# Output through VectorE transposes of 32x32 squares, in place of TensorE transposes; softmax weights normalised ahead of their split

## The chip, the cores and the metric

The kernel runs on one core of a Trainium2 chip. The metric is the device time of one execution in microseconds (us). The kernel before takes 1753.84 us, the median of 3 runs (1751.6 to 1754.51).

## The reference

Two stages run one after the other, in float32. The first is an induced attention in two steps, for 4 batches of 12480 tokens with 128 channels and 32 inducing rows. The second is a feed-forward layer with a squared ReLU, 128 to 2048 to 128.

```python
def mab(q, kv):
    s = scale * (q @ kv.transpose(0, 2, 1))
    s = s - s.max(-1, keepdims=True)
    a = np.exp(s)
    a /= a.sum(-1, keepdims=True) + 1e-09
    return a @ kv
h = mab(I, x)            # (4, 32, 128): the inducing rows attend to all tokens
y = mab(x, h)            # (4, 12480, 128): each token attends to the 32 rows of h
f = np.maximum(y @ w_in, 0.0)
out = (f * f) @ w_out    # 49920 tokens, 128 channels
```

## The kernel before, in words

**Units and blocks.** Each batch is cut into 13 units of 960 tokens, 52 units in all. A unit is two blocks (k = 0, 1) of 480 tokens, so the whole run has 104 blocks. Tokens lie along the free dimension in the feed-forward part, and channels lie on the 128 partitions.

**First.** For each unit, x is loaded to `xn` (120 partitions, 8 groups of 128 channels; line 383), turned to `xt` (128 channels x 960 tokens) by TensorE transposes (line 402), and evicted by ACT or DVE (`copy`, line 238). The scores of the 32 inducing rows, their running maximum and sum, and the running mix follow. When all units of a batch are done, `first_end` forms h and folds it into the first weight: `hw` = h times w_in, held as a high and a low part, so that the second attention and the first feed-forward matmul become one product.

**Second.** For each unit the 32 scores per token are formed (line 613), evicted (`ss`), turned (`s2t`, line 630), and then go through maximum, difference `d` and exponential (lines 637 to 644). The exponentials, not yet divided by their sum, are split into a high and a low part `sk` (lines 664 and 668), turned back (`ap`, line 675), evicted to `sw` (line 238, on ACT or DVE) and spread over 128 partitions by four transfers of the SP queue into `st` (line 690). The sum `z` goes another way: DVE sums it (line 648), POOL adds 1e-9 and squares it (lines 651 and 655), DVE inverts it (`zz`, line 659).

**The feed-forward block (`ffn_block`).** A block has four quads. A quad is four matmuls `h` from `st` (line 770), two ReLUs on ACT (`g`, line 778), one square on ACT (line 789), a high part `hi` and a low part `lo` on DVE (lines 793 and 797), and twelve matmuls into `op` (line 810): hi x wo_hi, hi x wo_lo, lo x wo_hi. One block therefore has 64 matmuls of 128x128 by 480. Since ReLU and square are homogeneous, the undivided weights make the result too large by z squared, which the end of the block takes out.

**The end of a block.** `op` (128 channels x 480 tokens, PSUM) is copied to `ot` by ACT or DVE (line 238), turned by four TensorE transposes to `otp` (line 830), multiplied by `zz` per token on DVE into `osb` (line 838), and once per unit stored by one transfer of 120 rows of 4096 bytes (line 845).

**What sets the order.** The whole program is written as tasks with an engine (or a choice `ACT|DVE`), an assumed duration, a due time, needs and buffers. `Plan.run` places them one after the other by these numbers, picks the engine where there is a choice, and the instructions are then issued in that order. Each engine executes its own queue in order. A changed task therefore moves others, and changes which engine the copies of line 238 go to. Two PSUM banks of kind `m` are shared by all narrow steps, and `ot`, `osb`, `st` and `sw` have two buffers each.

Of the kernel before, what the change touches and what calls it, by code (L numbers as in the profile page):

```python
# [154 lines left out]
def induced_attention_then_squared_relu_ffn(  # L155
# [448 lines left out]
    class Second:  # L604
# [6 lines left out]
        def score(self, where):  # L611
            for q in range(Q):
                nc.tensor.matmul(  # L613
                    where[q * M:(q + 1) * M, :], self.s["hT"][:, :M],
                    self.s["xt"][self.u][:, q * 2 * TS:(q + 1) * 2 * TS], start=True, stop=True,
                )

        def weigh(self, scored, where, bank_, due, step):
# [31 lines left out]
            def norm1():  # L650
                nc.gpsimd.tensor_scalar(v["z"], v["z"], 1e-9, 0.0, ALU.add, ALU.add)  # L651

            def norm2():
                v["zz"] = tiny.tile([TS, G, 1], F32, tag="z3", name=f"z3_{n}")
                nc.gpsimd.tensor_mul(v["zz"], v["z"], v["z"])  # L655

            def norm3():
# [1 line left out]
                nc.vector.reciprocal(s["zz", u], v["zz"])

# [43 lines left out]
            th = add("DVE", 210, high, d + 3 * step, [tp], port=True)  # L704
            tl = add("DVE", 335, low, d + 3 * step, [th], port=True)
            t = add("DVE", 330, total, d + 4 * step, [tp])
            t = add("POOL", 150, norm1, d + 5 * step, [t])
            t = add("POOL", 150, norm2, d + 5 * step, [t])
            self.zz = add("DVE", 120, norm3, d + 6 * step, [t])
            t = add("PE", 460, back, d + 4 * step, [tl], takes=[ba])  # L710
# [216 lines left out]
```

## Time and profile before

| | before |
|---|---|
| median of 3 runs | 1753.84 us (1751.6 to 1754.51) |
| profiled execution, first to last instruction | 1752.5 us |
| TensorE matmuls (PE) busy | 1724.4 us, 98% |
| VectorE (DVE) busy | 1666.2 us, 95% |
| ScalarE (ACT) busy | 1635.2 us, 93% |
| GpSimd (POOL) busy | 148.5 us, 8% |
| DMA, mean share of 16 engines (main queue) | 18.6%, 33416 packets |
| mean granted TensorE clock | 0.991 |

The profile gives one execution's span, and no separate time for that execution; the span lies 1.3 us under the median of the runs. Busy time of an engine is the time in which at least one of its instructions runs. Consecutive instructions on DVE overlap by some hundredths of a microsecond, so the means of the single instructions add up to more than the busy time. PE's matmul ends are modelled.

### The profile page before, as it was taken

What the parts mean: (1) busy time and instruction counts of PE and PEld (TensorE: products, weight loads), DVE (VectorE), ACT (ScalarE), POOL (GpSimd) and SP (SyncE); (2) the same over time, 40 slices, a digit from 0 to 9 for tenths busy, and PEclk for the clock granted to TensorE, in tenths of its full rate; (3) what the DMA queues carried; (4) which work ended last, traced back from release to release, by engine and by line L of the source; (5) the groups of instructions that cost most, each with busy time, mean ns of one, the idle gap of its engine ahead of it and who ended that gap; (6) DMA issues with size and microseconds to landing.
All of it is one profiled execution on the core that took longest, in us unless ns stands there. A gap on an engine that the chain in (4) does not pass through costs nothing.

```text
span 1752.5 us, 24391 instructions
## 1 busy us (share of the span) xinstructions
PE 1724.4 (98%) x9625; PEld 1418.5 (81%) x9625; DVE 1666.2 (95%) x1720; ACT 1635.2 (93%) x1677; POOL 148.5 (8%) x126
## 2 busy tenths in 40 slices
PE   7799999999999999999999999999999999999998
PEld 4488888888888888888888888888887888888886
DVE  6699999999999999999999999999999999999997
ACT  6599999999999999999999999999999999999997
POOL 1210010100100100100100100100110101010110
PEclk9699999999999999999999999999999999999999
DMA  9211211211121211211201211212101101010110
GB/s 236 64 46 34 57 46 34 57 46 37 44 57 35 57 45 39 63 36 46 68 23 46 53 38 46 57 34 50 42 24 34 35 23 46 24 45 24 35 35 23
DMA packets 33530, 82.46 MB, mean 47 GB/s; under 512 B 5032, under 2 KB 20424, under 8 KB 33416
## 3 DMA queue, kind: packets, MB, share of 16 engines
q1 hardware_dynamic: 33416, 80.91, 18.6%
q8 instruction: 76, 1.25, 0.3%
q14 instruction: 38, 0.31, 0.1%
HBM read 29.77 MB, written 25.56 MB: 32 GB/s over the span
## 4 chain that ended last, share of the span: by engine, by line
PE 95%; DMA 2%; DVE 1%; ACT 1%; issue 0%; SPq 0%; ACTq 0%; DVEq 0%
PE op L810 63%; PE h L770 21%; PE otp L830 3%; PE xtp L402 2%; PE na L613 2%; DMA words_i<-in_moe_w_in_dram 1%; PE ap L675 1%; PE nb L471 1%; PE wp L573 1%; PE na L417 1%; PE s2t L630 1%; PE ep L451 1%; DMA words_o<-in_moe_w_out_dram 0%; ACT g L778 0%; PE hp L471 0%
## 5 line engine op out<-in xcount | busy, mean ns | idle before, releaser
L797 DVE TENSOR_TENSOR lo<-g,hi 128x1920 fp32r<-128x1920 f32 x416 | 895.5, 2153 | 19.1 <-PE op L810 0.5
L778 ACT ACTIVATE g<-h 128x960 f32<-128x960 f32 x832 | 788.0, 970 | 53.1 <-PE h L770 44.4
L789 ACT ACTIVATE g<-g 128x1920 f32<-128x1920 f32 x416 | 755.6, 1816 | 9.7
L770 PE MATMUL h<-st,hw 128*128 128x480 f32 x1664 | 520.5, 386 | 2.5 <-DMA st<-sw 1.7
L793 DVE CAST hi<-g 128x1920 fp32r<-128x1920 f32 x416 | 479.4, 1152 | 23.8 <-ACT g L789 22.3
L810 PE MATMUL op<-hi,wo_hi 128*128 128x480 f32 x1664 | 477.8, 384 | 0.9 <-DVE hi L793 0.9
L810 PE MATMUL op<-lo,wo_hi 128*128 128x480 f32 x1664 | 471.1, 394 | 0.5 <-DVE lo L797 0.5
L810 PE MATMUL op<-hi,wo_lo 128*128 128x480 f32 x1664 | 431.7, 380 | 0.0
L770 PEld LDWEIGHTS h<-st,hw 128*128 128x128 f32 x1664 | 306.9, 188 | 65.8 <-ACT g L778 17.4
L810 PEld LDWEIGHTS op<-hi,wo_lo 128*128 128x128 f32 x1664 | 311.8, 188 | 50.9
L810 PEld LDWEIGHTS op<-hi,wo_hi 128*128 128x128 f32 x1664 | 305.2, 188 | 51.0 <-issue 1.8
L810 PEld LDWEIGHTS op<-lo,wo_hi 128*128 128x128 f32 x1664 | 292.9, 188 | 53.4 <-issue 11.8
L651 POOL TENSOR_SCALAR z<-z 120x8 f32<-120x8 f32 x52 | 89.6, 1723 | 1478.1 <-DVE z L648 1478.1
L838 DVE TENSOR_TENSOR osb<-otp,zz 120x512 f32<-120x512 f32 x104 | 71.3, 686 | 9.0 <-PE otp L830 8.8
L402 PE MATMUL xtp<-ident,xn 120*128 120x120 f32 x416 | 61.9, 273 | 5.8 <-DMA xn<-in_x_dram 4.8
L402 PEld LDWEIGHTS xtp<-ident,xn 120*128 120x128 f32 x416 | 49.8, 143 | 19.5 <-issue 5.8
L830 PE MATMUL otp<-ident,ot 128*120 128x128 f32 x416 | 62.4, 272 | 0.6 <-ACT ot L238 0.6
L830 PEld LDWEIGHTS otp<-ident,ot 128*120 128x120 f32 x416 | 50.9, 137 | 14.1 <-issue 1.4
L238 ACT COPY xt<-xtp 128x480 f32<-128x480 f32 x52 | 28.8, 559 | 14.3 <-PE xtp L402 13.6
L655 POOL TENSOR_TENSOR z<-z 120x8 f32<-120x8 f32 x52 | 37.7, 724 | 4.3
L675 PEld LDWEIGHTS ap<-identr,sk 120*128 120x128 f32 x208 | 31.3, 191 | 4.2 <-DVE hw L582 1.3
L238 DVE COPY ot<-op 128x480 f32<-128x480 f32 x53 | 34.5, 651 | 0.0
(94 smaller groups left out, 752.0 us busy)
## 6 DMA issues: line engine op xcount, KB each, us to landing
xn<-in_x_dram SPq DMA_DIRECT2D x52, 480.0 KB, 4.3
st<-sw SPq DMA_DIRECT2D x208, 120.0 KB, 2.3
out_dram<-osb SPq DMA_DIRECT2D x52, 480.0 KB, 3.3
words_i<-in_moe_w_in_dram SPq DMA_DIRECT2D x4, 512.0 KB, 10.2
words_o<-in_moe_w_out_dram SPq DMA_DIRECT2D x4, 512.0 KB, 7.6
ind_sb<-in_inducing_dram SPq DMA_DIRECT2D x1, 16.0 KB, 1.6
```

What stands on the lines that cost most here:

```text
L238: ENG[task.by](dst, src)
L402: nc.tensor.transpose(v["tp"][:, t * TS:(t + 1) * TS], self.xn[:, 4 * k + t, :], ident[:TS, :TS])
L651: nc.gpsimd.tensor_scalar(v["z"], v["z"], 1e-9, 0.0, ALU.add, ALU.add)
L675: nc.tensor.matmul(ap[:, q * TS:(q + 1) * TS], v["sk"][:, q].rearrange("t k a m -> t (k a m)"), identr[:TS, :TS], start=(q == 0), stop=(q ...
L770: nc.tensor.matmul(c["hp"][:, l, :BLK], s["hw"][:, f * P:(f + 1) * P], s["st", u][:, k, :], start=True, stop=True,)
L778: nc.scalar.activation(v["g"][:, 2 * i:2 * i + 2, :], c["hp"][:, :, :BLK], AF.Relu)
L789: nc.scalar.activation(v["g"], v["g"], AF.Square)
L793: nc.vector.tensor_copy(v["hi"], v["g"])
L797: nc.vector.tensor_sub(v["lo"], v["g"], v["hi"])
L810: nc.tensor.matmul(w["op"][:, :BLK], wo[:, 4 * j + l, :], v[name][:, l, :], start=(j == m == l == 0), stop=(j == NQ - 1 and m == 2 and l = ...
L830: nc.tensor.transpose(tp[:TS, q * P:(q + 1) * P], w["ot"][:, q * TS:(q + 1) * TS], ident)
L838: nc.vector.tensor_mul(s["osb", u].rearrange("t (q k) c -> t k q c", k=2)[:, k], w["tp"][:TS, :].rearrange("t (q c) -> t q c", q=Q), s["zz ...
```

## The change

It has four parts.

1. The x tokens are dealt to the partitions in another way. Before, partition p of a unit held 8 consecutive tokens, one piece of 4096 bytes. Now group j holds 120 consecutive tokens, so one load reads 8 pieces of 512 bytes per partition, and a block of 480 columns of `xt` is 480 consecutive tokens. The scores of the second attention read `xt` in two stretches of 120 columns for each matmul.
2. The softmax weights are divided by their sum ahead of their split: DVE adds 1e-9 to `z` (`safe`), inverts it (`invert`) and multiplies `d` by it (`share`, 120x256). The two POOL steps go, and one DVE reciprocal takes the place of another. The split, `ap`, `sw` and `st` now come behind these steps.
3. The end of a block is one DVE instruction: it transposes the 32x32 squares of `op` from PSUM into `rows` (128x480). The copy to `ot`, the four TensorE transposes and the multiplication by `zz` go.
4. The store of a block is four transfers, one for each group of 32 partitions. Each writes 480 pieces of 128 bytes: a quarter of the 512 bytes of each of 480 tokens. Before there was one transfer per unit.

```diff
-    XT, OT, ST = ("ACT|DVE", "ACT|DVE"), ("ACT|DVE", "ACT|DVE"), "ACT|DVE"
+    XT, ST = ("ACT|DVE", "ACT|DVE"), "ACT|DVE"
...
-    x_v = x.rearrange("b (p j) c -> b p j c", p=TS)
-    out_v = out.rearrange("(b p j) c -> b p j c", b=B, p=TS)
+    x_v = x.rearrange("b (u j p) c -> b u p j c", j=NT, p=TS)
+    out_v = out.rearrange("(b u k g r) (q c) -> b u k q r g c", b=B, u=NU, k=2, r=M, c=M)
...
-                nc.sync.dma_start(self.xn, x_v[b, :, u * NT:(u + 1) * NT, :])
+                nc.sync.dma_start(self.xn, x_v[b, u])
...
-                    where[q * M:(q + 1) * M, :], self.s["hT"][:, :M],
-                    self.s["xt"][self.u][:, q * 2 * TS:(q + 1) * 2 * TS], start=True, stop=True,
+                    where[q * M:(q + 1) * M, :].rearrange("m (k t) -> m k t", k=2), self.s["hT"][:, :M],
+                    self.s["xt"][self.u].rearrange("c (k q t) -> c q k t", k=2, q=Q)[:, q],
...
-            def norm1():
-                nc.gpsimd.tensor_scalar(v["z"], v["z"], 1e-9, 0.0, ALU.add, ALU.add)
-
-            def norm2():
-                v["zz"] = tiny.tile([TS, G, 1], F32, tag="z3", name=f"z3_{n}")
-                nc.gpsimd.tensor_mul(v["zz"], v["z"], v["z"])
-
-            def norm3():
-                s["zz", u] = tiny.tile([TS, G, 1], F32, tag="zz", name=f"zz_{n}")
-                nc.vector.reciprocal(s["zz", u], v["zz"])
+            def safe():
+                nc.vector.tensor_scalar_add(v["z"], v["z"], 1e-9)
+
+            def invert():
+                v["rz"] = tiny.tile([TS, G, 1], F32, tag="rz2", name=f"rz2_{n}")
+                nc.vector.reciprocal(v["rz"], v["z"])
+
+            def share():
+                nc.vector.tensor_mul(v["d"], v["d"], v["rz"].broadcast_to([TS, G, M]))
...
-        def done():
-            w["ot"] = att.tile([P, BLK], F32, tag="ot", name=f"ot_{n}")
-            copy(td, w["ot"], w["op"][:, :BLK])
-
-        def turn():
-            w["tp"] = tp = bank(f"otp_{n}")
+        def rows():
+            w["rows"] = att.tile([P, BLK // M, M], F32, tag="rows", name=f"rows_{n}")
+            nc.vector.transpose(w["rows"].rearrange("p g c -> p (g c)"), w["op"][:, :BLK])
+
+        def store():
             for q in range(Q):
-                nc.tensor.transpose(
-                    tp[:TS, q * P:(q + 1) * P], w["ot"][:, q * TS:(q + 1) * TS], ident
-                )
-
-        def turned():
...
-            nc.vector.tensor_mul(
-                s["osb", u].rearrange("t (q k) c -> t k q c", k=2)[:, k],
-                w["tp"][:TS, :].rearrange("t (q c) -> t q c", q=Q),
-                s["zz", u][:, k * Q:(k + 1) * Q].broadcast_to([TS, Q, C]),
-            )
-
-        def store():
-            nc.sync.dma_start(out_v[b, :, u * NT:(u + 1) * NT, :], s["osb", u])
...
+                nc.sync.dma_start(out_v[b, u, k, q], w["rows"][q * M:(q + 1) * M])
```

The plan moves other work with it. In the names below the first numbers are the unit and the block (and the quad), and the last number only counts tiles. Over the whole run, 14 of the copies to `xt` and 12 of the casts to `sw` go from DVE to ACT: DVE had 52 and 15 of them and has 38 and 3; ACT had 52 and 37 and has 66 and 49.

The first place is DVE while block 0 of unit 7 runs, where the softmax of unit 8 is finished (`d`, `z`, `zz` or `rz`, `sk`). Before:

```order
L664 CAST sk_8_3270<-d_8_3251 120x8x32
L838 TENSOR_TENSOR osb_6_3085<-otp_6_1_3261,zz_6_2711 120x4x128
L668 TENSOR_TENSOR sk_8_3270<-d_8_3251,sk_8_3270 120x8x32
L648 TENSOR_REDUCE z_0_8_3283<-d_8_3251 120x8
L797 TENSOR_TENSOR lo_7_0_2_3286<-g_7_0_2_3202,hi_7_0_2_3259 128x1920
L793 CAST hi_7_0_3_3312<-g_7_0_3_3255 128x1920
L238 COPY xt_9_3314<-xtp_9_0_3315 128x480
L659 RECIPROCAL zz_8_3333<-z_0_8_3325 120x8
L797 TENSOR_TENSOR lo_7_0_3_3335<-g_7_0_3_3255,hi_7_0_3_3312 128x1920
L793 CAST hi_7_1_0_3349<-g_7_1_0_3301 128x1920
```

Now:

```order
L644 TENSOR_REDUCE z_0_8_3225<-d_8_3212 120x8
L791 TENSOR_TENSOR lo_7_0_2_3230<-g_7_0_2_3153,hi_7_0_2_3216 128x1920
L647 TENSOR_SCALAR z_0_8_3225<-z_0_8_3225 120x8
L787 CAST hi_7_0_3_3247<-g_7_0_3_3210 128x1920
L651 RECIPROCAL rz_0_8_3260<-z_0_8_3225 120x8
L233 COPY xt_9_3249<-xtp_9_0_3250 128x480
L654 TENSOR_TENSOR d_8_3212<-d_8_3212,rz_0_8_3260 120x256
L791 TENSOR_TENSOR lo_7_0_3_3270<-g_7_0_3_3210,hi_7_0_3_3247 128x1920
L658 CAST sk_8_3288<-d_8_3212 120x8x32
L787 CAST hi_7_1_0_3290<-g_7_1_0_3243 128x1920
L662 TENSOR_TENSOR sk_8_3288<-d_8_3212,sk_8_3288 120x8x32
```

Before, the split `sk` followed the exponential at once, and the sum came behind it. Now the sum, `safe`, `invert` and `share` come first, with a `lo`, a `hi` and another `lo` between them, and the two steps of the split `sk` stand around the first `hi` of block 1.

The second place is PE from `ap` of unit 8 on, which opens the way of that unit's weights through `sw` and `st` to its first `h`. Before (the first `h_8` stands 14 rows behind the last row shown, 60 matmuls of 480 columns and three groups of transposes after `ap_8`):

```order
L675 MATMUL ap_8_3288<-identr,sk_8_3270 128x120 x4
L810 MATMUL op_7_0_3188<-hi_7_0_2_3259,wo_hi 128x480 x2
L810 MATMUL op_7_0_3188<-hi_7_0_2_3259,wo_lo 128x480 x4
L770 MATMUL h_7_1_1_3303<-st_7_2994,hw_881 128x480 x2
L402 MATMUL xtp_9_0_3315<-ident,xn_9_2847 128x120 x4
L810 MATMUL op_7_0_3188<-lo_7_0_2_3286,wo_hi 128x480 x4
L770 MATMUL h_7_1_2_3328<-st_7_2994,hw_881 128x480
L810 MATMUL op_7_0_3188<-hi_7_0_3_3312,wo_hi 128x480 x2
L770 MATMUL h_7_1_2_3328<-st_7_2994,hw_881 128x480
L810 MATMUL op_7_0_3188<-hi_7_0_3_3312,wo_hi 128x480 x2
L810 MATMUL op_7_0_3188<-hi_7_0_3_3312,wo_lo 128x480 x4
L770 MATMUL h_7_1_3_3346<-st_7_2994,hw_881 128x480 x2
```

Now:

```order
L669 MATMUL ap_8_3308<-identr,sk_8_3288 128x120 x4
L804 MATMUL op_7_1_3305<-hi_7_1_0_3290,wo_hi 128x480 x2
L804 MATMUL op_7_1_3305<-hi_7_1_0_3290,wo_lo 128x480 x4
L764 MATMUL h_7_1_5_3325<-st_7_3000,hw_881 128x480 x2
L804 MATMUL op_7_1_3305<-lo_7_1_0_3303,wo_hi 128x480 x4
L764 MATMUL h_7_1_6_3344<-st_7_3000,hw_881 128x480 x2
L804 MATMUL op_7_1_3305<-hi_7_1_1_3333,wo_hi 128x480 x4
L804 MATMUL op_7_1_3305<-hi_7_1_1_3333,wo_lo 128x480 x4
L764 MATMUL h_7_1_7_3360<-st_7_3000,hw_881 128x480 x2
L804 MATMUL op_7_1_3305<-lo_7_1_1_3347,wo_hi 128x480 x4
L764 MATMUL h_8_0_0_3370<-st_8_3327,hw_881 128x480 x2
```

`ap` has moved later by half a block: 28 matmuls of 480 columns stand between it and the first `h_8`. Over the 52 units this number is 27 to 45 in the first three batches (60 to 62 before), 24 or 32 in the last (64 to 66 before), and 20, 20 and 16 at the first units of the later batches (42, 38 and 41 before).

The third place is the queue of SP, which issues all transfers. Before:

```order
L690 DMA st_6_2683<-sw_6_2675 64x480 x4
L383 DMA xn_9_2847<-in_x_dram 120x1024
L845 DMA out_dram<-osb_5_2792 120x1024
L690 DMA st_7_2994<-sw_7_2983 64x480 x4
L383 DMA xn_10_3184<-in_x_dram 120x1024
L845 DMA out_dram<-osb_6_3085 120x1024
L690 DMA st_8_3305<-sw_8_3297 64x480 x4
```

Now:

```order
L684 DMA st_6_2692<-sw_6_2682 64x480 x4
L823 DMA out_dram<-rows_5_0_2718 32x15x32 x4
L378 DMA xn_9_2788<-in_x_dram 120x8x128
L823 DMA out_dram<-rows_5_1_2874 32x15x32 x4
L684 DMA st_7_3000<-sw_7_2991 64x480 x4
L823 DMA out_dram<-rows_6_0_3026 32x15x32 x4
L378 DMA xn_10_3137<-in_x_dram 120x8x128
L823 DMA out_dram<-rows_6_1_3161 32x15x32 x4
L684 DMA st_8_3327<-sw_8_3317 64x480 x4
```

Each block's store stands in the queue as four transfers. The store of block 1 stands ahead of the four `st` of the unit after the next, and the store of block 0 right behind them; a load of x stands between the two stores.

More of the change, by code (lines that the diff above doesn't have):

```diff
@@ L613, in score @@
                 nc.tensor.matmul(
-                    where[q * M:(q + 1) * M, :], self.s["hT"][:, :M],
-                    self.s["xt"][self.u][:, q * 2 * TS:(q + 1) * 2 * TS], start=True, stop=True,
+                    where[q * M:(q + 1) * M, :].rearrange("m (k t) -> m k t", k=2), self.s["hT"][:, :M],
+                    self.s["xt"][self.u].rearrange("c (k q t) -> c q k t", k=2, q=Q)[:, q],
+                    start=True, stop=True,
                 )
@@ L703, in weigh @@
             tp = add("ACT", 307, power, d + 2 * step, [td])
[L704 to L710, printed above, removed]
-            ts = add(ST, (455, 565), stacked, d + 5 * step, [t], takes=[bw], reads=[ba])
-            self.ready = add("SP", 1000, spread, d + 6 * step, [ts], takes=[self.bst], reads=[bw])
+            t = add("DVE", 330, total, d + 3 * step, [tp])
+            t = add("DVE", 70, safe, d + 3 * step, [t])
+            t = add("DVE", 115, invert, d + 3 * step, [t])
+            t = add("DVE", 340, share, d + 4 * step, [t], port=True)
+            th = add("DVE", 210, high, d + 4 * step, [t], port=True)
+            tl = add("DVE", 335, low, d + 5 * step, [th], port=True)
+            t = add("PE", 460, back, d + 5 * step, [tl], takes=[ba])
+            ts = add(ST, (455, 565), stacked, d + 6 * step, [t], takes=[bw], reads=[ba])
+            self.ready = add("SP", 1000, spread, d + 7 * step, [ts], takes=[self.bst], reads=[bw])
     def narrow(second, f, g, due, step, begun=None):
@@ L821, in ffn_block @@
             last = quad(j, last)
-        def done():
-            w["ot"] = att.tile([P, BLK], F32, tag="ot", name=f"ot_{n}")
-            copy(td, w["ot"], w["op"][:, :BLK])
-        def turn():
-            w["tp"] = tp = bank(f"otp_{n}")
-            for q in range(Q):
-                nc.tensor.transpose(
-                    tp[:TS, q * P:(q + 1) * P], w["ot"][:, q * TS:(q + 1) * TS], ident
-                )
-        def turned():
-            if k == 0:
-                s["osb", u] = att.tile([TS, NT, C], F32, tag="osb", name=f"osb_{b}_{u}")
-            nc.vector.tensor_mul(
-                s["osb", u].rearrange("t (q k) c -> t k q c", k=2)[:, k],
-                w["tp"][:TS, :].rearrange("t (q c) -> t q c", q=Q),
-                s["zz", u][:, k * Q:(k + 1) * Q].broadcast_to([TS, Q, C]),
-            )
-        def store():
-            nc.sync.dma_start(out_v[b, :, u * NT:(u + 1) * NT, :], s["osb", u])
-        bt = Buffer("m")
-        end = t0 + PERIOD / 2 + 8000
-        td = add(OT[k], (455, 570), done, end + 1500, [last], reads=[bo], late=LATE_OT)
-        t = add("PE", 420, turn, end + 3000, [td], takes=[bt])
-        t = s["out", u, k] = add("DVE", 600, turned, end + 4000, [t, second.zz], reads=[bt])
-        if k == 1:
-            add("SP", 2000, store, end + 6000, [t, s["out", u, 0]])
+        def rows():
+            w["rows"] = att.tile([P, BLK // M, M], F32, tag="rows", name=f"rows_{n}")
+            nc.vector.transpose(w["rows"].rearrange("p g c -> p (g c)"), w["op"][:, :BLK])
+        def store():
+            for q in range(Q):
+                nc.sync.dma_start(out_v[b, u, k, q], w["rows"][q * M:(q + 1) * M])
+        br = Buffer("rows")
+        end = t0 + PERIOD / 2 + 8000
+        t = add("DVE", 570, rows, end + 1500, [last], reads=[bo], late=LATE_OT, takes=[br])
+        add("SP", 2000, store, end + 4000, [t], reads=[br])
         return w["begun"]
```

6 lines of the change are left out of this document (1 added, 5 removed).

## The prediction

> **What bounds the kernel now.** I read the busy shares first, then the chain of waits, then the waits of each engine, all for the stretch from 120 to 1700 us, where every unit looks alike and 99 of the 104 blocks end.
>
> ```profile
> 120.00:1700.00 1580.00, 1580.00 (x8673) 1314.95 (x8672) 1533.15 (x1526) 1512.00 (x1494) 127.65 (x103) 1.00 0.17 43
> by line: PE op L810 66.4%; PE h L770 22.1%; PE otp L830 2.7%; PE xtp L402 1.9%; PE na L613 1.7%; PE ap L675 1.2%; PE nb L471 1.0%; PE na L417 0.9%; PE s2t L630 0.7%; PE wp L573 0.7%; PE ep L451 0.5%; PE hp L471 0.1%; PE htp L556 0.0%; PE ht
> 853.55 1.75 PE op L810 x8
> ```
>
> In the first row the columns after the length are PE, PEld, DVE, ACT and POOL busy, the granted clock, the DMA share and GB/s. PE is busy all 1580 us at full clock, and the chain (second row) lies on PE throughout: PE sets the time. But DVE is busy 1533.15 us, and what is left of it, 46.85 us, is not all free:
>
> ```profile
> DVE hi L793 <- ACT g L789: 19.0, 51, 0.8
> DVE osb L838 <- PE otp L830: 6.3, 17, 0.4
> DVE lo L797 <- PE op L810: 0.5, 1, 0.5
> DVE hacc L483 <- PE hp L471: 0.3, 1, 0.3
> DVE sk L664 <- ACT d L644: 0.3, 1, 0.3
> ACT g L778 <- PE h L770: 43.3, 151, 0.7
> ```
>
> DVE waits for another engine for only 26.4 us (the first five rows). The other 20.4 us are short gaps between its own instructions. A DVE that never waited for others would need 1533.15 + 20.4 = 1553.6 us. PE has slack of its own: eight matmuls of 480 columns take 1.75 us (0.2188 each), 99 blocks x 64 make 1386 us, while `op` and `h` hold 88.5% of 1580 = 1398. So PE alone needs about 1568 us, DVE 1554, and together they take 1580: 12 us over the slower. Two engines sit at the limit, and work must leave both.
>
> **PE.** The four transposes of a block go.
>
> ```profile
> 101.35 0.44 PE otp L830 x4
> L830 PE MATMUL otp<-ident,ot 128*120 128x128 f32 x416 | 62.4, 272 | 0.6 <-ACT ot L238 0.6
> ```
>
> The 62.4 us count overlapping ends. On the chain a block's group takes 0.44 us; 2.7% of 1580 is 42.7 us for 99 blocks, the same 0.43. PE alone comes to 1568 - 43 = 1525 us. The scores read `xt` in two stretches instead of one, with as many columns; I take nothing for it.
>
> **DVE.** These groups lose instructions, or show what the new ones cost:
>
> ```profile
> L838 DVE TENSOR_TENSOR osb<-otp,zz 120x512 f32<-120x512 f32 x104 | 71.3, 686 | 9.0 <-PE otp L830 8.8
> L238 DVE COPY ot<-op 128x480 f32<-128x480 f32 x53 | 34.5, 651 | 0.0
> L238 DVE COPY xt<-xtp 128x480 f32<-128x480 f32 x52 | 33.9, 653 | 0.5
> L238 DVE CAST sw<-ap 128x480 fp32r<-128x480 f32 x15 | 9.7, 649 | 0.0
> L641 DVE TENSOR_TENSOR d<-s2t,mx 120x256 f32<-120x256 f32 x52 | 22.0, 422 | 1.3
> L659 DVE RECIPROCAL zz<-z 120x8 f32<-120x8 f32 x52 | 10.2, 195 | 0.1
> L438 DVE TENSOR_SCALAR neg<-mx 128x1 f32<-128x1 f32 x4 | 0.6, 148 | 0.0
> L487 DVE COPY hacc<-nb 128x128 f32<-128x128 f32 x3 | 0.9, 286 | 0.1
> L238 ACT COPY ot<-op 128x480 f32<-128x480 f32 x51 | 28.3, 555 | 5.3 <-PE op L810 5.3
> L238 ACT COPY xt<-xtp 128x480 f32<-128x480 f32 x52 | 28.8, 559 | 14.3 <-PE xtp L402 13.6
> L238 ACT CAST sw<-ap 128x480 fp32r<-128x480 f32 x37 | 20.5, 554 | 0.4 <-PE ap L675 0.4
> ```
>
> Removed: 71.3 (`osb`) + 34.5 (`ot`) + 14 x 0.653 (`xt` moved to ACT) + 12 x 0.649 (`sw` moved) = 122.7 us. Added: `share` 52 x 0.422 = 21.9; `safe` 52 x 0.17 = 8.8 (between the 0.148 and 0.195 of the small rows); one reciprocal replaces another. The 104 transposes are in no trace. From below, one is a copy of the same 128x480 from PSUM, 0.651 us. From above, I let each element cost twice: the copies of 480 and 128 columns differ by 0.365 us for 352 columns, so 480 more make 0.498 and the whole 1.149. I take 0.69, near the copy, since nothing but the order of the elements changes: 71.8 us. Net 102.5 - 122.7 = -20.2 us; for 99 of 104 blocks -19.2, and DVE alone comes to 1554 - 19 = 1534 us (1530 to 1580 between the bounds).
>
> The Trainium skill, "VectorE: DVE Perf Modes", The three transpose paths, lists 311 ns for a 128x128 VectorE transpose in bf16. That is 25 ns over the 286 ns of the copy above; by it one transpose here would be about 0.676 us (an estimate) and DVE alone 1.4 us less.
>
> **ACT** loses 28.3 us and takes on 14 x 0.559 + 12 x 0.554 = 14.5, net -13.8: it stays third. POOL's two steps were on no chain; their end only fed `zz`.
>
> **The longer softmax.** In the order `ap` now stands 28 to 42 matmuls ahead of the next unit's first `h` instead of 60, so `sw` and `st` have 28 x 0.2188 = 6.1 us where they had 13 or more.
>
> ```profile
> 804.39 0.55 PE L675 MATMUL ap<-identr,sk 120*128 120x120 f32 x4
> 805.27 0.65 DVE L238 CAST sw<-ap 128x480 fp32r<-128x480 f32 x1
> 805.95 3.13 SPq L690 DMA_DIRECT2D st<-sw  x4
> L690 SPq DMA_DIRECT2D st<-sw x208: 461/589/1718, 71.9 to 1697.5; - x104
> DMA to landing us min/median/max: 2.1/2.3/4.1
> L648 DVE TENSOR_REDUCE z<-d 120x8 f32<-120x256 f32 x52 | 21.5, 413 | 0.0
> L789 ACT ACTIVATE g<-g 128x1920 f32<-128x1920 f32 x416 | 755.6, 1816 | 9.7
> L797 DVE TENSOR_TENSOR lo<-g,hi 128x1920 fp32r<-128x1920 f32 x416 | 895.5, 2153 | 19.1 <-PE op L810 0.5
> L793 DVE CAST hi<-g 128x1920 fp32r<-128x1920 f32 x416 | 479.4, 1152 | 23.8 <-ACT g L789 22.3
> 74.87 1.94 PE h L770 x4
> ```
>
> From the end of `ap` (804.8, where the next matmul starts) the first transfer goes out 1.15 us later, the second 0.6 behind it, and that one lands 2.3 later: 4.1 us; block 0 needs only these two. It is covered in the usual unit, with 2 us over. Ahead of the first `h` of the three later batches stand 20, 20 and 16 matmuls (3.5 to 4.4 us): I add 1.5 us for them. At the very first unit nothing covers it: sum 0.41, `safe`, `invert` and `share` come onto the chain where before only the split was, about 1.2 us plus gaps: +1.5.
>
> **The transfers.** Pieces, by stretches in which one kind of transfer is alone:
>
> ```profile
> 53.00:56.00 3.00, 1.13 (x10) 0.27 (x2) 2.89 (x5) 0.61 (x3) 2.78 (x3) 0.50 0.57 175
> 802.00:805.00 3.00, 3.00 (x19) 2.68 (x18) 3.00 (x4) 2.96 (x4) 0.62 (x1) 1.00 0.60 164
> 806.00:811.00 5.00, 5.00 (x27) 4.32 (x26) 5.00 (x5) 4.97 (x5) 0.00 (x0) 1.00 0.46 102
> 829.00:832.00 3.00, 3.00 (x16) 2.53 (x15) 3.00 (x8) 2.83 (x7) 0.00 (x0) 1.00 0.64 164
> 5.00:48.00 43.00, 35.94 (x410) 22.25 (x411) 30.97 (x79) 28.45 (x79) 7.68 (x6) 0.99 1.00 249
> ```
>
> The first is a weight load of 2048 pieces of 512 bytes: 0.57 x 3 = 1.71 us of all 16 engines, 13.4 ns per piece on its engine. The second is the store before (120 pieces of 4096 bytes, 240 ns each), the third the four `st` (256 of 1920 bytes, 2.3 us, 144 ns each), the fourth a load of x (1.92 us). A block's store is now 1920 pieces of 128 bytes, 120 per engine. At 13.4 ns that is 1.6 us, at 144 ns 17.3. The 512-byte row is the nearest in size; I take twice its price, a margin for writing short pieces: 27 ns, 3.2 us per block of 16 us, beside other work. It reaches the path only where stores, `st` and x fill a unit's 31.9 us (1580 / 49.5): (31.9 - 2.3 - 1.9) / 240 = 115 ns per piece. The store of block 1 is some 14 us ahead of the next `st` in the order of DVE (three `lo`, four `hi` and 3 us of small steps between `rows` and the end of the split), so it is gone by then. Loads of x in 512-byte pieces cost no more than before by the weight row; from 5 to 48 us, where DMA is full, 16 of them may save or lose some 5 us. I take nothing.
>
> **The sum.** DVE at 1534 us becomes the slower engine, PE at 1525 is 9 us below it. Before, the two stood 14 us apart and lost 12; closer together I take 16: 1550 us, 30 less than 1580. For 52 units instead of 49.5 that is 31.5; with +3 for the softmax the profiled 1752.5 becomes 1724, and the median, 1.3 above the span, 1725 us.
>
> **Rivals.** *PE alone decides* (chance 0.13): transposes at the copy's price and x loads that land earlier let PE have all it sheds: 1752.5 - 104 x 0.435 = 1707, median 1709. For it: most of DVE's waits are for ACT, which in turn waits 43.3 us for PE's `h`, so they shrink with PE. Against it: in a stretch of 1580 - 43 = 1537 us DVE at 1530 would have 7 us to spare, half of what it has now.
>
> *The weights come late* (0.13): if `sw`, now on ACT in most units, waits behind a whole square (1.8 us) and the transfers queue for 0.9 us more, 4.1 us becomes 6.8. PE then stalls 0.7 us in the 14 units with 27 or 28 matmuls, 1.55 in the 6 with 24, 2.4 in the 2 with 20 and 3.3 in the one with 16: 27 us, nearly all that is saved, 1751. For it: the margin fell from 9 us to 2. Against it: both delays would have to meet in every unit.
>
> *Transposes at half rate* (0.12), the slower side: DVE alone 1533.15 + 20.4 + 0.95 x (119.5 + 30.7 - 122.7) = 1580, with 16 us on top 1596; 16 x 1.05 + 3 = 20 us more, 1774. It decides from where the saving is used up: 28.5 / 1.05 = 27 in the stretch, 0.69 + 27/99 = 0.96 us per transpose. Against it: nothing in the trace shows a DVE instruction on 32-bit elements from PSUM below the copy's rate.
>
> *DMA decides* (0.07): at 144 ns a unit's transfers take 34.6 + 2.3 + 1.9 = 38.8 us; 52 of them and the 75 us ahead of the first `h` give about 2090 us. By the Trainium skill, "DMA: Bandwidth & Descriptors", Specifications, a transfer needs pieces of 512 bytes for line rate, and below that a read-modify-write is made. No run so far shows it; at double the 512-byte price it stays hidden, it decides only from the 115 ns above.
>
> **How the numbers follow.** The forecast itself (0.55) spans 1712 to 1745: 10 us for a friction of 6 to 26, 5 for the transposes, 5 for the start. The range 1705 to 1757 takes in the first two rivals and leaves out the last two. This kernel's measurement tells no change from one of 0.2% (3.5 us). Faster: 0.55 + 0.13 and part of the late weights, 0.72. Same 0.08. Slower 0.20.
>
> **What would show it.** Right: in the same stretch DVE over 98% with its waits for ACT nearly gone, PE with first gaps at `op` waiting for `hi` or `lo`, `rows` at 0.65 to 0.72 us, DMA share 0.2 to 0.35, `h` not waiting for `st`. Wrong: `rows` over 0.96 us; `h` waiting for `st` by tens of us; DMA share near 1 or stores landing after 10 us and more; ACT as the busiest.

## The result, and the profile after

The changed kernel takes 1722.9 us, the median of 4 runs (1722.4 to 1723.9), beside 1754.0 us for the kernel before (1751.6 to 1754.5). The ratio is 0.982, with a 95% interval of 0.981 to 0.984. The forecast was 1725 us. It came this close by luck: two errors cancel, which the profile shows at once. Among the later kernels two executions ran at a mean granted clock of 0.305 and 0.654 and took 5294 and 2294 us; the times below leave them out.

The span is cut into three parts by the first and the last matmul into `h`. In these rows of the view of one tile's instructions, the two times after the durations are the starts of the first and the last one. Before:

```profile
L770 PE MATMUL h<-st,hw x1664: 373/380/782, 74.9 to 1737.3; 128*128 128x480 f32 x185
```

After:

```profile
L764 PE MATMUL h<-st,hw x1664: 372/381/782, 82.0 to 1707.8; 128*128 128x480 f32 x185
```

| us | before | after | difference | forecast |
|---|---|---|---|---|
| start, up to the first `h` | 74.9 | 82.0 | +7.1 | +1.5 |
| steady part, first to last `h` | 1662.4 | 1625.8 | -36.6 | -31.5, +1.5 |
| rest, up to the end of the span | 15.2 | 13.2 | -2.0 | 0 |
| span | 1752.5 | 1721.0 | -31.5 | -28.5 |

The start cost 5.6 us more than was thought, the steady part gave 6.6 us more and the end 2. Next come rows of the page of after: busy time, share and count of each engine, the main DMA queue, and the chain of waits by engine; the last row is the chain of the page of before.

```profile
PE 1682.7 (98%) x9209; PEld 1381.8 (80%) x9209; DVE 1630.8 (95%) x1745; ACT 1607.2 (93%) x1652; POOL 22.5 (1%) x22
...
q1 hardware_dynamic: 276412, 80.93, 23.8%
...
PE 76%; ACT 8%; DVE 7%; issue 4%; DMA 0%; DVEq 0%; ACTq 0%; SPq 0%
```

```profile
PE 95%; DMA 2%; DVE 1%; ACT 1%; issue 0%; SPq 0%; ACTq 0%; DVEq 0%
```

PE's busy time fell by 41.7 us, DVE's by 35.4, ACT's by 28.0. The shares of these three are what they were, to the per cent. What changed is the chain: it lay on PE for 95%, and now for 76%; the rest is mostly on ACT, on DVE and in what the view calls issue, time in which an engine waited for nothing that the profile shows. The groups of the changed kernel show what the new instructions cost (behind the bar the busy time in us and the mean of one in ns):

```profile
L791 DVE TENSOR_TENSOR lo<-g,hi 128x1920 fp32r<-128x1920 f32 x416 | 896.5, 2155 | 15.6
L787 DVE CAST hi<-g 128x1920 fp32r<-128x1920 f32 x416 | 477.4, 1147 | 31.2 <-ACT g L783 23.1 <-PE na L412 4.7
L819 DVE STREAM_TRANSPOSE rows<-op 128x480 f32<-128x480 f32 x104 | 70.3, 676 | 1.3 <-PE op L804 1.2
L654 DVE TENSOR_TENSOR d<-d,rz 120x256 f32<-120x256 f32 x52 | 21.8, 419 | 0.0
L647 DVE TENSOR_SCALAR z<-z 120x8 f32<-120x8 f32 x52 | 8.6, 166 | 0.1
```

A transpose of 128x480 takes 676 ns (0.69 was taken), `share` 419 ns and `safe` 166 ns. Two windows with one kind of transfer alone (columns as in the prediction) price the transfers, and the stretch of the prediction stands under them:

```profile
851.00:857.00 6.00, 6.00 (x31) 5.02 (x29) 6.00 (x10) 5.94 (x8) 0.00 (x0) 1.00 0.26 41
845.50:851.00 5.50, 5.50 (x35) 4.65 (x28) 5.49 (x11) 4.96 (x7) 0.00 (x0) 1.00 0.37 89
120.00:1700.00 1580.00, 1574.85 (x8436) 1309.01 (x8437) 1532.48 (x1575) 1520.43 (x1505) 5.55 (x3) 1.00 0.22 43
```

The store of a block is 0.26 x 6 = 1.56 us of all 16 engines, 13 ns for each of the 120 128-byte pieces on its engine; a load of x is 0.37 x 5.5 = 2.04 us (1.92 before), 34 ns for each of the 60 512-byte pieces. DVE is busy 97.0% of the stretch, as before; it did not become full. Nor did its waits for ACT go away. These are the longest rows of the view of waits, of each engine in turn (us in total, times, longest), from 120 to 1680 us:

```profile
PEld h L764 <- ACT g L772: 23.2, 81, 0.7
PEld op L804 <- DVE lo L791: 8.3, 23, 1.0
ACT g L772 <- PE h L764: 41.8, 81, 1.6
DVE hi L787 <- ACT g L783: 20.8, 33, 1.3
```

The first two in the kernel before, in the same window:

```profile
PEld h L770 <- ACT g L778: 14.8, 68, 0.4
PEld op L810 <- DVE lo L797: 4.5, 16, 0.3
```

PE (at its weight loads) waits for ACT and DVE, ACT for PE, DVE for ACT. The last two waits are hardly changed (42.6 and 19.0 before); what is new is that PE waits longer: 8.4 us more for ACT, 3.8 more for `lo`, and 4.3 for `hi` where it was 0.2. Weight loads overlap matmuls, so not all of this is lost time. A stretch of the chain with far less of PE than the mean shows how the path leaves PE (start, length, what):

```profile
170.06 0.44 PE h L764 x2
...
171.35 0.45 PE h L764 x2
...
171.82 0.97 ACT g L772
172.80 1.71 ACT g L783
174.50 0.02 issue
174.53 1.17 DVE hi L787
...
177.87 1.15 DVE hi L787
179.02 0.32 DVE mx L425
...
181.32 0.15 DVE neg L431
181.47 0.33 DVE ss L233
...
181.84 0.94 ACT g L772
```

At 171.8 the path leaves PE: a ReLU, a square, `hi`, then small steps of the softmaxes on DVE (`mx`, `neg`, `ss`), and a ReLU again. Two pieces of about 2 us among the lines left out are called issue; by DVE's timeline a `lo` runs in each. For these 10 us no PE instruction sets the pace.

### The profile page after: what moved, and what is told of

Read it like the earlier page. It is cut to its first block, busy times and chain, and to the rows that moved or that the text cites. A ratio compares the mean times of both kernels' runs of the same rounds, so it can differ in the third digit from the quotient of the medians.

```text
span 1721.0 us, 24111 instructions
## 1 busy us (share of the span) xinstructions
PE 1682.7 (98%) x9209; PEld 1381.8 (80%) x9209; DVE 1630.8 (95%) x1745; ACT 1607.2 (93%) x1652; POOL 22.5 (1%) x22
## 3 DMA queue, kind: packets, MB, share of 16 engines
q1 hardware_dynamic: 276412, 80.93, 23.8%
## 4 chain that ended last, share of the span: by engine, by line
PE 76%; ACT 8%; DVE 7%; issue 4%; DMA 0%; DVEq 0%; ACTq 0%; SPq 0%
PE op L804 52%; PE h L764 18%; ACT g L772 4%; ACT g L783 3%; DVE hi L787 3%; DVE lo L791 2%; PE xtp L397 1%; PE na L608 1%; PE ap L669 1%; PE nb L466 1%; PE na L412 1%; PE s2t L626 0%; DVE hw L577 0%; PE ep L446 0%; ACT d L640 0%
## 5 line engine op out<-in xcount | busy, mean ns | idle before, releaser
L783 ACT ACTIVATE g<-g 128x1920 f32<-128x1920 f32 x416 | 754.2, 1813 | 8.2
L787 DVE CAST hi<-g 128x1920 fp32r<-128x1920 f32 x416 | 477.4, 1147 | 31.2 <-ACT g L783 23.1
L804 PE MATMUL op<-lo,wo_hi 128*128 128x480 f32 x1664 | 440.7, 384 | 1.5 <-DVE lo L791 1.5
L804 PEld LDWEIGHTS op<-lo,wo_hi 128*128 128x128 f32 x1664 | 307.0, 188 | 58.5 <-DVE lo L791 9.9
L804 PEld LDWEIGHTS op<-hi,wo_hi 128*128 128x128 f32 x1664 | 299.2, 188 | 50.8 <-issue 6.2
L819 DVE STREAM_TRANSPOSE rows<-op 128x480 f32<-128x480 f32 x104 | 70.3, 676 | 1.3 <-PE op L804 1.2
L233 ACT COPY xt<-xtp 128x480 f32<-128x480 f32 x66 | 36.6, 556 | 16.8 <-PE xtp L397 16.6
L669 PEld LDWEIGHTS ap<-identr,sk 120*128 120x128 f32 x208 | 31.5, 193 | 4.7 <-ACT xt L233 1.5
L608 PE MATMUL na<-xt,hT 128*32 128x240 f32 x416 | 32.7, 387 | 0.0
L669 PE MATMUL ap<-identr,sk 120*128 120x120 f32 x208 | 29.4, 265 | 1.2 <-DVE sk L662 1.2
L233 ACT CAST sw<-ap 128x480 fp32r<-128x480 f32 x49 | 27.3, 557 | 1.7 <-PE ap L669 1.7
L446 PE MATMUL ep<-ident,e 128*120 128x128 f32 x104 | 20.7, 281 | 4.9 <-ACT e L438 4.4
L233 DVE COPY xt<-xtp 128x480 f32<-128x480 f32 x38 | 24.2, 638 | 1.0 <-PE xtp L397 1.0
```

The source lines that it names most:

```text
L233: ENG[task.by](dst, src)
L446: nc.tensor.transpose(v["ep"][:TS, k * P:(k + 1) * P], v["e"][:, k * TS:(k + 1) * TS], ident)
L608: nc.tensor.matmul(where[q * M:(q + 1) * M, :].rearrange("m (k t) -> m k t", k=2), self.s["hT"][:, :M], self.s["xt"][self.u].rearrange("c ...
L669: nc.tensor.matmul(ap[:, q * TS:(q + 1) * TS], v["sk"][:, q].rearrange("t k a m -> t (k a m)"), identr[:TS, :TS], start=(q == 0), stop=(q ...
L783: nc.scalar.activation(v["g"], v["g"], AF.Square)
L787: nc.vector.tensor_copy(v["hi"], v["g"])
```

## The experiments

The expectations name the theories by letters and say what each holds. Differences to the changed kernel are between medians; the kernel before took 1753.7 to 1754.6 us beside every group of runs, and such a difference is good to about 3 us. "First to last" is the steady part of the table above.

### Is the longer start due to the layout of x?

The kernel before, with 512-byte pieces both in its loads and in its stores:

```diff
-    x_v = x.rearrange("b (p j) c -> b p j c", p=TS)
-    out_v = out.rearrange("(b p j) c -> b p j c", b=B, p=TS)
+    x_v = x.rearrange("b (u j p) c -> b u p j c", j=NT, p=TS)
+    out_v = out.rearrange("(b u j p) c -> b u p j c", b=B, u=NU, j=NT)
...
-                nc.sync.dma_start(self.xn, x_v[b, :, u * NT:(u + 1) * NT, :])
+                nc.sync.dma_start(self.xn, x_v[b, u])
...
-            nc.sync.dma_start(out_v[b, :, u * NT:(u + 1) * NT, :], s["osb", u])
+            nc.sync.dma_start(out_v[b, u], s["osb", u])
```

> The kernel before with part 1 alone: x is loaded and the output stored in 512-byte pieces (8 tokens of a partition lie 120 tokens apart), everything else as before; the result is the reference's. The changed kernel reached its first h at 82.0 us instead of 74.9, and DMA stayed full until 55 us instead of 48. Theory A (the 512-byte loads cost the start those 7 us): first h at 80 to 82 us, 1759 to 1762 us in all. Rival B (the longer softmax ahead of the first st costs them): first h at 75 us, 1754 us.

Measured: 1758.5 us, a ratio of 1.0025 (1.0015 to 1.0034) to the kernel before. The first and last `h` of this kernel, and then its window in which DMA is full:

```profile
L770 PE MATMUL h<-st,hw x1664: 372/380/785, 78.1 to 1740.1; 128*128 128x480 f32 x185
```

```profile
5.00:48.00 43.00, 34.53 (x402) 21.63 (x406) 27.99 (x73) 27.51 (x75) 5.91 (x5) 1.00 1.12 226
```

The same window, and the one after it, of the changed kernel:

```profile
5.00:48.00 43.00, 34.49 (x368) 21.39 (x368) 26.39 (x70) 25.66 (x71) 5.21 (x4) 0.94 1.10 223
50.00:55.00 5.00, 3.03 (x50) 1.86 (x48) 4.49 (x10) 3.52 (x11) 2.20 (x2) 1.00 0.98 188
```

The layout alone makes the start 3.2 us longer and leaves the steady part as it was (1662.0). With 512-byte pieces the 16 engines, full in all three (a share of 1.00 before, 1.10 and 1.12 here), move 223 to 226 GB/s instead of 249. In the changed kernel that leaves 26 x 43 = 1.1 MB for later, 5 us at 223 GB/s, and DMA is still full from 50 to 55 us (a share of 0.98, and 0.31 before). So it is shown that the layout costs time, 2.6 to 6.0 us by the interval and all of it outside the steady part. It is about half of what theory A expected; the 3.2 us of the start are from one profile, and starts scatter by as much (next section).

### What does the division cost by itself?

The kernel before with the division ahead of the split; its last DVE step becomes a plain copy, and `safe` and `invert` stand ahead of `share` as in the change (the plan moved 48 `xt` and 32 `ot` copies to ACT, and 19 `sw` casts to DVE):

```diff
+            def share():
+                nc.vector.tensor_mul(v["d"], v["d"], v["rz"].broadcast_to([TS, G, M]))
...
-            nc.vector.tensor_mul(
+            nc.vector.tensor_copy(
                 s["osb", u].rearrange("t (q k) c -> t k q c", k=2)[:, k],
                 w["tp"][:TS, :].rearrange("t (q c) -> t q c", q=Q),
-                s["zz", u][:, k * Q:(k + 1) * Q].broadcast_to([TS, Q, C]),
             )
```

> The kernel before with part 2 alone: the weights are divided ahead of their split, and the last DVE step of a block only copies the turned result. PE does all it did. The plan moves 48 copies of xt and 32 of ot from DVE to ACT and 19 casts of sw the other way: DVE loses some 9 us in sum, ACT gains some 34. Theory A (the plan balances, PE at 1568 us alone still decides): 1752 to 1762 us, with the first h 1 to 2 us later. Rival B (the longer softmax brings the weights late): 1765 us and more, with h waiting for st by tens of us.

Measured: 1761.2 us, 1.004 (1.0025 to 1.0055) of the kernel before. That is theory A's range. The first `h` is 1.8 us later (76.7), the steady part 5.7 us longer (1668.1). On its page the chain lies on ACT for 28% (1% before), which took over 61 copies and casts in sum; whether the 5.7 us are the division's or theirs was not tried apart. The layout's 3.2 and these 1.8 make 5.0 of the 7.1 us of the start. The rest, and each of the two by itself, is within the scatter: five kernels with the same start (the changed one and the last four below) reached their first `h` between 78.8 and 82.0 us, at 80.6 in the mean, 5.7 behind the kernel before.

### Does DVE set the time of the changed kernel?

The changed kernel without the division, which is left out and not done elsewhere. The plan also moves nine `xt` copies and one `sw` cast to ACT. The means of DVE's groups sum to 66 us less; its busy time, which counts overlaps once, falls by 32 us to 1598.9.

```diff
-            t = add("DVE", 330, total, d + 3 * step, [tp])
-            t = add("DVE", 70, safe, d + 3 * step, [t])
-            t = add("DVE", 115, invert, d + 3 * step, [t])
-            t = add("DVE", 340, share, d + 4 * step, [t], port=True)
-            th = add("DVE", 210, high, d + 4 * step, [t], port=True)
+            th = add("DVE", 210, high, d + 4 * step, [tp], port=True)
```

> The changed kernel without the sum, safe, invert and share of the softmax (52 each on DVE): the weights go into the split undivided and nothing divides later, so the output lacks the normalisation of the second attention. DVE loses about 68 us (62 of these steps, the rest by copies that the plan moves to ACT). Theory A (DVE is the slower engine of the changed kernel and sets the time): 1706 to 1712 us, where PE alone decides. Rival B (PE already decides, DVE's load is hidden): 1719 to 1724 us. Rival C (all three engines hold each other up): in between, 1713 to 1718.

Measured: 1722.8 us, ratio 0.982 (0.980 to 0.983): no change. What DVE had saved it waited away, as its row in the waits of this kernel (120 to 1680 us) says:

```profile
DVE hi L783 <- ACT g L779: 48.9, 117, 1.4
```

That is 48.9 us where the changed kernel had 20.8. So DVE's own work was not what set the time. The ten instructions that moved to ACT (5.6 us) blur this a little, as ACT has 21% of this kernel's chain, 8% in the changed one:

```profile
PE 66%; ACT 21%; issue 7%; DVE 4%; DMA 2%; POOL 0%; SPq 0%; ACTq 0%; DVEq 0%; POOLq 0%
```

What less work on DVE gives with every instruction in its place stands in the last experiment.

Now the other way round: each transpose is made twice, the second into a tile that nothing reads.

```diff
             nc.vector.transpose(w["rows"].rearrange("p g c -> p (g c)"), w["op"][:, :BLK])
+            twice = att.tile([P, BLK], F32, tag="twice", name=f"twice_{n}")
+            nc.vector.transpose(twice, w["op"][:, :BLK])
```

> The changed kernel with a second, unread transpose of the same squares on DVE in every block: DVE does 104 x 0.676 = 70 us more, as if one transpose took 1.35 us. Theory A (DVE is at its limit): DVE alone comes to 1598 us in the steady stretch, with 12 to 16 us on top 1612; 1785 to 1797 us in all. Rival B (DVE has 40 us and more of room behind PE): 1730 to 1755 us.

Measured: 1765.0 us, 1.0057 (1.0042 to 1.0072) of before, 42 us more than the changed kernel for 67 us of instructions (104 x 640 ns; 57 of busy time). That fits neither theory. The chain of this kernel from 120 to 1680 us, and then the longest of PE's waits:

```profile
by line: PE op L804 19.7%; DVE lo L791 13.7%; DVE hi L787 13.1%; issue 11.7%; ACT g L783 7.4%; ACT g L772 7.3%; PE h L764 5.8%; DVE rows L819 3.6%; DVE twice L821 3.3%; DMA st<-sw 2.6%; PE na L608 1.0%; DVE mx L633 1.0%; DVE d L637 0.9%; SP
```

```profile
PEld op L804 <- DVE hi L787: 43.5, 91, 0.9
```

Here DVE has more of the chain than PE, and PE waits 43.5 us for `hi` (4.3 in the changed kernel). About two thirds of the load are paid: DVE doesn't decide in the changed kernel, but it is close to it.

### Is it PE that gave the gain?

The changed kernel with four idle TensorE transposes of a constant per block, into a bank that nothing reads:

```diff
+        def turn():
+            tp = bank(f"otp_{n}")
+            for q in range(Q):
+                nc.tensor.transpose(tp[:TS, q * P:(q + 1) * P], ident[:, :TS], ident)
...
+        add("PE", 420, turn, end + 3000, [t], takes=[Buffer("m")])
```

> The changed kernel with four TensorE transposes per block kept, of a constant and into a bank that nobody reads: PE does the 104 x 0.43 us again, DVE and ACT do nothing for it. Theory A (the gain is the work that left PE, cut by DVE's limit): PE alone at 1568 us in the steady stretch again, 1750 to 1760 us in all. Rival B (DVE sets the time of the changed kernel and PE has room): 1725 to 1735 us.

Measured: 1758.2 us, 1.0022 (1.0013 to 1.0031) of before: 35.3 us more than the changed kernel, and a steady part of 1661.6, the one before. The whole steady gain is gone though the instructions of DVE, ACT and POOL keep what they saved (in sum within 2 us; the plan moves two copies and two casts to ACT), and the chain (120 to 1680 us) is back on PE:

```profile
by line: PE op L804 64.3%; PE h L764 21.7%; PE otp L828 2.7%; PE xtp L397 1.9%; PE na L608 1.7%; PE ap L669 1.2%; PE nb L466 1.0%; issue 1.0%; PE na L412 0.9%; ACT g L772 0.8%; PE wp L568 0.6%; PE s2t L626 0.6%; PE ep L446 0.5%; DVE hi L787
```

So the transposes' leaving PE is what the gain needs. 104 x 0.435 = 45 us of them were worth 35.

### Do the short pieces hold up the weights?

Each store is cut into four transfers of 32-byte pieces, 16 transfers per block:

```diff
             for q in range(Q):
-                nc.sync.dma_start(out_v[b, u, k, q], w["rows"][q * M:(q + 1) * M])
+                for h in range(4):
+                    sl = slice(h * M // 4, (h + 1) * M // 4)
+                    nc.sync.dma_start(out_v[b, u, k, q, :, :, sl], w["rows"][q * M:(q + 1) * M, :, sl])
```

> The changed kernel with each store cut into four transfers of 32-byte pieces: four times the pieces (480 per DMA engine and block) and 16 issues per block. In the changed kernel a block's store took some 2.1 us of all engines, 17.5 ns per piece. Theory A (a piece has a fixed price and the stores stay hidden until they fill the block's 15.6 us): about 8.4 us per block, DMA share 0.55 to 0.65, 1719 to 1730 us. Rival B (short writes cost more the shorter they are, or the issues block st): over 1740 us, h waiting for st.

Measured: 1746.6 us, 0.9956 (0.9941 to 0.9971) of before, 24 us more than the changed kernel. The main queue of this kernel, the longest wait of PE, two rows of SP's timeline at a change of the batch, and a window behind them:

```profile
q1 hardware_dynamic: 895420, 81.01, 35.9%
```

```profile
PE h L764 <- DMA st<-sw: 12.0, 3, 5.8
```

```profile
906.38 8.22 SPq L825 DMA_DIRECT2D out_dram<-rows  x16
914.70 2.39 SPq L684 DMA_DIRECT2D st<-sw  x4
```

```profile
918.00:923.00 5.00, 5.00 (x13) 4.11 (x13) 0.00 (x0) 2.77 (x4) 0.00 (x0) 0.50 0.06 13
```

The DMA share is far under the 0.55 to 0.65 that was expected, which went by 17.5 ns per piece where the store alone, above, gives 13. Four times as many pieces took (0.359 x 1745.9 - 0.238 x 1721.0) x 16 = 3470 us more, 5.8 ns for each added piece. The weights were late all the same, at the changes of the batch: `h` waits there for `st`, because SP first issues the 16 stores of a block, 0.5 us each and 8.2 in all, where the changed kernel has four, and the `st` transfers stand behind them. The lateness comes from the issues on SP and not from the pieces. The waits make 12 of the 24 us. Behind them the granted clock was 0.50 for some us (last row): PE got through 13 matmuls in 5.00 us, 0.385 each in place of 0.2188. Windows of 5 us behind the other two waits have 0.68 and 0.51; for the three places that makes some 6 us (an estimate, 3 x 13 x 0.166). The end is longer too: from the last `h` to the end of the span 19.7 us (1745.9 - 1726.2) in place of 13.2.

### Would larger x pieces be better?

An attempt at a faster version, against the longer start: x is loaded in 2048-byte pieces, so the tokens lie in another order in `xn`; the evictions to `xt` put them right by writing 16 bytes apart, and the first scores read `xt` at that spacing:

```diff
-    x_v = x.rearrange("b (u j p) c -> b u p j c", j=NT, p=TS)
+    x_v = x.rearrange("b (u k p j) c -> b u p k j c", u=NU, k=2, p=TS)
...
-                copy(e, self.xt[:, k * BLK:(k + 1) * BLK], v["tp"][:, :BLK])
+                copy(
+                    e, self.xt[:, k * BLK:(k + 1) * BLK].rearrange("c (p j) -> c j p", j=4),
+                    v["tp"][:, :BLK].rearrange("c (j p) -> c j p", j=4),
+                )
```

> The changed kernel with x loaded in pieces of 2048 bytes (4 tokens of one partition lie together); the copies to xt put the columns back into token order (writes 16 bytes apart), and the first scores read them at that stride. The result is the reference's. Theory A (512-byte loads cost the start 5 to 7 us, the strides nothing): DMA full until 48 to 50 us, first h at 75 to 77 us, 1716 to 1719 us. Rival B (strided writes or reads cost ACT, DVE or PE): copies to xt above 0.60 us or scores slower, 1723 us and more.

Measured: 1747.2 us, 0.996 (0.9946 to 0.9974) of before, 24 us slower than the changed kernel. The groups of this kernel, and behind them the same of the changed one:

```profile
L233 ACT COPY xt<-xtp 128x480 f32<-128x480 f32 x66 | 68.2, 1043 | 14.1 <-PE xtp L397 14.0
L233 DVE COPY xt<-xtp 128x480 f32<-128x480 f32 x38 | 38.2, 1006 | 0.2 <-PE xtp L397 0.2
L416 PE MATMUL na<-xt,indT 128*32 128x240 f32 x312 | 40.8, 602 | 0.1
```

```profile
L233 ACT COPY xt<-xtp 128x480 f32<-128x480 f32 x66 | 36.6, 556 | 16.8 <-PE xtp L397 16.6
L233 DVE COPY xt<-xtp 128x480 f32<-128x480 f32 x38 | 24.2, 638 | 1.0 <-PE xtp L397 1.0
L412 PE MATMUL na<-xt,indT 128*32 128x240 f32 x312 | 23.4, 372 | 0.1
```

The copies took 1043 and 1006 ns instead of 556 and 638, and the matmuls 602 instead of 372. That adds 32, 14 and 17 us to three engines, and the steady part is 23.6 us longer (1649.4). The start was not shorter (first `h` at 82.7), though DMA was no longer full from 50 to 55 us (a share of 0.39, 0.98 in the changed kernel). Whether the slower copies took there what the loads gave was not tried apart.

### What is a microsecond worth on each engine?

Four kernels keep the order of the changed one and only make instructions of one kind shorter. Less on DVE: the transpose handles 128 of the 480 columns (the other columns of the output stay zero), 308 ns each, 38 us in all.

```diff
-            nc.vector.transpose(w["rows"].rearrange("p g c -> p (g c)"), w["op"][:, :BLK])
+            nc.vector.transpose(w["rows"][:, :4].rearrange("p g c -> p (g c)"), w["op"][:, :P])
```

> The changed kernel in the same order on every engine, but the transpose of a block takes only 128 of its 480 columns (the other columns of the output are zeros): by the slope of the copies (1.037 ns per column) DVE does 104 x 0.365 = 38 us less. Division alone taken away changed nothing, but the plan had moved copies with it; here nothing moves. Theory P (PE's own work decides, DVE is hidden): 1719 to 1723 us. Theory D (DVE sets the time, as the prediction had it): 1700 us or less. Theory M (the three engines hold each other up): 1710 to 1718.

Less on ACT: the square leaves out the last 40 columns, 1678 ns instead of 1813, 56 us in all.

```diff
-                nc.scalar.activation(v["g"], v["g"], AF.Square)
+                nc.scalar.activation(v["g"][:, :, :440], v["g"][:, :, :440], AF.Square)
```

> The changed kernel in the same order, but the square leaves out the last 40 of 480 columns (they stay unsquared in the output): 160 elements at 0.881 ns (the slope between the 970 ns of 960 elements and the 1813 ns of 1920), 416 times, ACT does 59 us less. Theory P (PE decides): 1717 to 1723 us. Theory A (ACT decides): 1680 us or less. Theory M (the engines hold each other up): 1705 to 1716.

Less on PE: the third product (lo) leaves out 40 columns, 1664 x 40 x 0.2188 / 480 = 30 us in all.

```diff
+                        n_ = 440 if m == 2 else BLK
...
-                                w["op"][:, :BLK], wo[:, 4 * j + l, :], v[name][:, l, :],
+                                w["op"][:, :n_], wo[:, 4 * j + l, :], v[name][:, l, :n_],
```

> The changed kernel in the same order, but the products of the low part leave out the last 40 of 480 columns (these columns lack the low part's small share): 1664 matmuls x 40 columns x 0.456 ns (0.2188 us per 480) = 30 us less on PE. Theory P (PE decides): 1692 to 1698 us. Theory M: 1703 to 1712. If another engine decides: 1717 to 1723.

Less on DVE and ACT: the first two edits together.

> The edits of less on DVE and less on ACT together, same order: DVE 38 us and ACT 59 us less, PE as in the changed kernel. It shows what PE needs when nobody holds it up. PE alone was worked out as 1525 us per 1580 us of the steady stretch before, 1605 us from the first to the last h, where the changed kernel takes 1626. Theory P with friction from the other two: about 20 us less, 1700 to 1706 us. If the 20 us are PE's own (waits inside PE that no other engine causes): 1717 to 1723.

| us | taken off | time | ratio to before (95%) | against the changed kernel | first to last |
|---|---|---|---|---|---|
| DVE | 38 | 1717.1 | 0.980 (0.978 to 0.982) | -6 | 1620.8 |
| ACT | 56 | 1715.9 | 0.979 (0.977 to 0.980) | -7 | 1620.1 |
| PE | 30 | 1709.5 | 0.975 (0.974 to 0.977) | -13 | 1613.9 |
| DVE and ACT | 38 and 56 | 1709.3 | 0.975 (0.974 to 0.977) | -14 | 1615.0 |

One row of the waits (120 to 1680 us) of each of the first three, in the order of the table:

```profile
DVE hi L791 <- ACT g L787: 36.3, 63, 1.4
```

```profile
ACT g L772 <- PE h L764: 71.0, 146, 1.9
```

```profile
PEld op L805 <- DVE hi L787: 17.3, 70, 0.4
```

An engine that gets less to do mostly waits more for its neighbour: DVE 36.3 us for ACT (20.8 in the changed kernel), ACT 71.0 for PE (41.8), PE 17.3 for `hi` (4.3). Every relief is worth something and none is worth its whole size: 0.44 us per us on PE, 0.15 on DVE, 0.12 on ACT. With differences good to 3 us, PE's is clearly the largest, and the other two can't be told apart. The first three times lie in the ranges of theory M, that on ACT at its edge. The fourth lies in neither of its two ranges: with DVE and ACT both lighter the steady part is 11 us shorter, about half of the 20 that the changed kernel loses against PE alone (next section). The other half is still there; of PE's waits the longest is still `h` for ACT, 16.2 us (23.2). So it is borne out that the three engines hold each other up, with PE weighing most. Between which single instructions the rest is lost was not tried, nor whether another order or more buffers would win it back.

## Why the prediction was right or wrong

**PE: right.** It said -43 us in the stretch, 45 over the run; PE's busy time fell by 41.7 over the run, and giving PE the same work back undid the whole steady gain.

**DVE's costs: right for the transposes, a little off in the sum.** A transpose took 676 ns where 0.69 us was taken, `share` 419 ns for 422, `safe` 166 for 170. The means of all DVE groups sum to some 27 us less than before, where the working has 20.2. Some old steps got shorter too: the copies to `xt` from 653 to 638 ns, `hi` from 1152 to 1147, `d` from 422 to 401; why is open. The Trainium skill, "VectorE: DVE Perf Modes", The three transpose paths, has 311 ns for 128x128 in bf16, from which the prediction estimated 0.676 us. The trace agrees, though in float32 from PSUM: 676 ns, and 308 ns for 128x128.

**The step that failed: "DVE at 1534 us becomes the slower engine".** With it fell "DVE over 98% with its waits for ACT nearly gone": DVE is busy 97.0%, and 20.8 us of these waits are left. PE's longest wait is at `h` for ACT (23.2 us), and not at `op` for `hi` or `lo` as it was said to be. By own work the step was no worse than a tie: with the measured sizes DVE alone needs about 1528 us (1554 less 0.95 x 27) beside PE's 1525. What failed is that the longer own work decides. With 32 us less busy time on DVE the time did not move, with 38 less in the same order it fell by 6; 67 us more of instructions cost only 42. No engine alone sets the time after the change; the chain goes from one to the next. That the sum held is in part luck: a friction of about the right size was put on the wrong base. For 99 blocks the steady 36.6 us are 34.8, so the stretch now takes 1580 - 34.8 = 1545 us: PE alone (1525) and 20 us more, where the prediction had DVE alone (1534) and 16.

**ACT "stays third": it was not free.** The means of its groups sum to 16 us less where 13.8 were worked out (its busy time, in which overlaps count once, fell by 28), but 56 us less on it still gave 7. An engine at 96% of the stretch (1520 of 1580) takes part in the loss.

**The start: the term that was mis-sized.** "I take nothing" for the x loads was wrong by 3.2 us; its bound of 5 us held. It rested on a row that was misread. The weight load from 53 to 56 us is not "2048 pieces of 512 bytes", which would be 1 MB: its 175 GB/s for 3 us are one load of 512 KB, and a row of `w_out` as the kernel reads it is 1024 bytes. So it is 512 pieces of 1024 bytes, 53 ns each (0.57 x 3 x 16 / 512), and not 13.4 ns for 512 bytes. A 512-byte piece of x took 34 ns: such a load is 6% dearer than before alone (2.04 us, 1.92 before), and when all engines are full they move 9 to 10% less (223 to 226 GB/s, 249 before). The softmax on the chain was forecast at +1.5 and measured 1.8, in one profile.

**The changes of the batch: wrong, 1.5 us for nothing.** In the changed kernel `h` waits for `st` only at the first unit. The margin is small, though: it was used up as soon as SP had more to issue.

**Stores: right that they are hidden, but by luck in the price.** The price was 27 ns a piece, twice the misread 13.4; measured were 13, 1.6 us per block. The row read rightly and doubled gives 107 ns, close under the 115 from which the stores would reach the path. The DMA share of 0.22 in the stretch, 23.8% over the run, lies in the 0.2 to 0.35 that were named. The Trainium skill, "DMA: Bandwidth & Descriptors", Specifications, has a read-modify-write below 512 bytes; no run shows a cost of it. A 128-byte piece of a store takes 13 ns, a 512-byte piece of a load 34: a fourth of the bytes in 0.38 of the time.

**The rivals.** *PE alone decides* (1709): PE weighs most, but the time is 14 us above the 1709, and 30 us less on PE gave 13. *The weights come late*: not in the changed kernel; the cut stores showed the mechanism with SP's issues as its cause. *Half rate* and *DMA decides* are ruled out by the 676 ns and the 13 ns.

## What to carry to other kernels

Where three engines are each busy over 95% and hand work to each other in a fixed order, don't look for the one that bounds the time after the change: take the longest own work, add at least the friction that the present kernel shows (12 us here before the change, 20 after it), and expect, as in this kernel, a microsecond taken from one engine to be worth a tenth to a half of itself, and one added to cost more than half. Before a row of the profile is used as a price per piece, hold pieces times size against the bytes that the row moved. A stretch in which DMA is full needs its own price for the size of the pieces: the loss there was 9 to 10%, and 6% in a quiet one. When a step moves closer to its deadline, count what stands ahead of it in the queue that issues its transfers.
